# Output-layer weight factors kept whole in DRAM and split on arrival, with later and more buffers for the activated values

## The chip, the cores and the metric

The kernel runs on one core of a Trainium2 chip. The metric is the time of one execution on the device, in microseconds (us), of that core. Before the change three runs took 1200.15, 1204.12 and 1204.95 us; the median is 1204.12 us.

## The reference, cut to what matters

A retention layer (attention with a decay per head) is followed by two feed-forward layers. All inputs are float32.

```python
for t in range(S):                       # B, H, S, D = 4, 8, 768, 64
    state = gamma * state + k[:, :, t] (outer) v[:, :, t]
    y[:, :, t] = scale * q[:, :, t] @ state
x = y reordered to (3072, 512)
h = x @ w_in;  x = maximum(0.01 * h, h) @ w_out          # 512 -> 2048 -> 512
h = x @ w2_in; out = (h * sigmoid(1.702 * h)) @ w2_out   # 512 -> 2048 -> 512
```

## The kernel before, in words

The program is unrolled. It has five stages: the retention layer, then for each of the two feed-forward layers (`lay` 0 and 1) `first` (`x @ w_in` and the activation) and `second` (`g @ w_out`).

Every matrix product is done by Winograd's scheme, with seven products of quarter matrices in place of eight. A quarter product is made of float32 numbers held as two parts, `hi` (rounded to the format `F32R`) and `lo` (the rest), so each takes three matmuls: hi by lo, hi by hi, lo by hi. The weights' seven combinations are called factors here. An SBUF tile `w` holds the factors of one `q` (one eighth of the hidden width) as `[P, 2, 2, 7, P]`: two halves, then hi and lo, then the seven factors of 128 x 128.

**Preparing weights.** `Prep` turns one half of a raw weight tile into seven factors, in steps that `later` runs a given number of ticks after the start: `load` (two DMAs on SP's queue), `words` (two operations of ACT, L122 and L123), `bits` (three of DVE, L127 to L131), `sums` (five of POOL, L136 and L141), `high_part` (ACT's cast to hi, L150), `low_part` (DVE's subtraction, L153) and `store` (L158 and L159, two DMAs of 448 KB to the DRAM tensor `wd`). With a `dest` the parts go straight to a `w` tile and nothing is stored. In `first`, `FAST` sets the ticks of the steps and `line` says which preparations are to come and how many ticks apart (`JIT`, `STORED`). In layer 0 that is 8 of the layer's own input weights 4.25 ticks apart, then the 16 of `w_out` and 8 of the second layer's `w2_in`, all 5.4 apart. In layer 1 it is 8 at 4.25 and the 16 of `w2_out` at 7.5.

**`first`.** The tokens are cut into four blocks of 768, and each into two halves of `T1` = 384 columns. For each block and each `q`, seven products of six matmuls (L410, 128 x 384) are made; after each comes one `tick`. An iteration `n` is one pair (block, q), and two of its seven products belong to the previous `n`. ACT copies and activates (L473; L416 in layer 0, the sigmoid L419 in layer 1), DVE adds banks (L437, L479) and in layer 1 multiplies by the sigmoid (L420). The activated values go into a tile `g` of the pool `g_p` (five buffers) and from there to the DRAM tensor `gd` by a DMA of 192 KB on ACT's queue (L434). In the last block, after the product that is the last to use the input weights of a `q`, `after(q)` takes the `w` tile over for the output weights of that `q` and loads them from `wd` (L692, 1792 KB on SP's queue). Three iterations before the end `prepared` opens the first buffers of `second` and loads eight tiles of `gd` (L536, SP's queue).

**`second`.** Three blocks of 1024 tokens, for each seven products over all eight `q`, 48 matmuls of 128 x 512 (L601). ACT casts each loaded tile to hi (L545) and DVE subtracts for lo (L550) and forms the blocks' sums (L576). The first product (tag `d`) goes through all eight `w` tiles, six matmuls each. Tiles of `gd` are loaded up to 13 items ahead, on SP's queue.

Order and waits: each engine and each DMA queue runs its instructions in the order in which the program issues them. A buffer is reused when the last reader of its former tile is done, for a `g` tile when its store has landed.

```python
            t = g_p.tile([P, T1], F32, tag="g", name="g")          # hidden(), before
    JIT, STORED = 4.25, (5.4, 7.5)
    FAST = (6, 7, 8, 12, 13, 15)
```

Of the kernel before, what the change touches and what calls it, by code (L numbers as in the profile page):

```python
# [9 lines left out]
F32 = mybir.dt.float32  # L10
# [44 lines left out]
class Later:  # L55


    def __init__(self):
        self.now = 0
        self.due = {}  # L60

    def at(self, ticks, step):
        self.due.setdefault(self.now + ticks, []).append(step)

    def tick(self):
        for step in self.due.pop(self.now, []):
            step()
        self.now += 1

    def drain(self):  # L70
        while self.due:
            self.tick()


@with_exitstack
def retention_two_ffn(ctx: ExitStack, tc: tile.TileContext, qkv, consts, small, w1i, w1o, w2i, w2o, scratch, out):
# [4 lines left out]

    wd = {(kind, lay): dram.tile([P, n, 2, 2, 7, P], F32, name=f"wd{kind}{lay}")
          for kind, lay, n in (("o", 0, NQ), ("i", 1, NQ // 2), ("o", 1, NQ))}
    gd = [dram.tile([KF, P, NT], F32, name=f"gd{lay}") for lay in range(2)]
# [6 lines left out]

    later = Later()

    class Prep:
# [288 lines left out]
    def first(lay, wt, blocks, g_p, prep, line, after, prepared):  # L385
# [3 lines left out]
        with ExitStack() as c:  # L389
# [23 lines left out]

            def act(src, dst):
                if lay == 0:
                    nc.scalar.activation(out=dst, in_=src, func=AF.Lrelu)  # L416
                else:
                    s = u_p.tile([P, T1], F32, tag="sg", name="sg", bufs=3)
                    nc.scalar.activation(out=s, in_=src, func=AF.Sigmoid, scale=1.702)  # L419
                    later.at(1, lambda: nc.vector.tensor_tensor(out=dst, in0=src, in1=s, op=ALU.mult))  # L420

            def hidden(n, r, f, src):

                blk, q = pairs[n]
                t = g_p.tile([P, T1], F32, tag="g", name="g")
                ticks = 0 if lay == 0 else 3
                if callable(src):
                    src(t)
                    later.at(1, lambda: act(t, t))
                    ticks += 1  # L430
                else:
                    act(src, t)
                cols = slice((2 * blk + r) * T1, (2 * blk + r + 1) * T1)
                later.at(ticks, lambda: nc.scalar.dma_start(out=gd[lay][f * NQ + q][:, cols], in_=t))  # L434

# [5 lines left out]
            for n in range(len(pairs) + 1):  # L441
# [57 lines left out]
                if now:  # L499
                    product(cur["a"], n, 2, False)  # L500
                    hidden(n, 0, 0, cur["a"])
                    form(2)
                    tick(free)
                    product(cur["b"], n, 7, False)
                    hidden(n, 1, 1, lambda t: add(t, cur["b"], cur["p"]))
                    form(7)
                    tick(free)
# [176 lines left out]

    def loader(kind, lay, n):

        tiles = []

        def after(q):
            t = w_tile(q)  # L690
            if q < n:
                nc.sync.dma_start(out=t.bitcast(F32), in_=wd[kind, lay][:, q])  # L692
            tiles.append(t)

        return tiles, after

    JIT, STORED = 4.25, (5.4, 7.5)

    line = ([(p, w1[p.q], JIT) for p, _ in line] + [(p, None, STORED[0]) for p in preps("o", 0)]
            + [(p, None, STORED[0]) for p in preps("i", 1)[:NQ]])  # L700
# [11 lines left out]

    tiles, after = loader("o", 0, NQ)
    first(0, w1, blocks, g_p, prep_p, line, after, lambda: prepared(0))
    right.close()
    tiles1, after = loader("i", 1, NQ // 2)
    right = ExitStack()
# [10 lines left out]
    g_p = right.enter_context(tc.tile_pool(name="g", bufs=5, side="right", reuse_waits="tile"))  # L728
    F_BUFS = 2
    ctx_p = ExitStack()  # L730
# [4 lines left out]
    for _ in range(3):  # L735
        later.tick()
    line = [(p, tiles1[p.q], JIT) for p in preps("i", 1)[NQ:]] + [(p, None, STORED[1]) for p in preps("o", 1)]
    tiles, after = loader("o", 1, NQ)
    first(1, tiles1, blocks, g_p, prep_p, line, after, lambda: prepared(1))
# [68 lines left out]
```

## Time and profile before

| | us |
|---|---|
| median of three runs | 1204.12 |
| the profiled execution | 1204.84 |
| its span (first to last instruction) | 1203.1 |
| TensorE (PE) busy | 1083.9 (90%) |
| VectorE (DVE) busy | 859.9 (71%) |
| ScalarE (ACT) busy | 579.5 (48%) |
| GpSimd (POOL) busy | 350.5 (29%) |
| granted TensorE clock, mean | 0.96 of full |
| moved by DMA | 263.09 MB, mean 219 GB/s |

`first` of layer 0 runs from about 119 to 399 us of the span, `second` of layer 0 to about 653, `first` of layer 1 from about 655 to 953, and `second` of layer 1 to about 1196. Busy shares are averages over these stages. A busy PE is not a PE at its full pace: matmuls are pipelined, and a matmul that is modelled to last longer counts as busy too. So a stage is best judged by its count of matmuls against the time that so many take in an undisturbed stretch.

### The profile page before, as it was taken

Reading aid. Unit: us, or ns where it says so; the run is one execution under the profiler, and the core shown is the slowest. Engines: PE = TensorE matmul, PEld = TensorE weight load, DVE = VectorE, ACT = ScalarE, POOL = GpSimd, SP = SyncE. Lnnn points to the kernel's source line nnn. Section 1 sums busy time; section 2 is a strip of 40 time slices with the busy share of each in tenths; the row PEclk is TensorE's granted clock in tenths of the full one; section 3 lists DMA queues with packets and bytes.
Section 4 is the critical chain, followed back from the end, with each engine's and each line's share of the span. In section 5 each row is a group of like instructions: output and inputs, shape, how many; then the busy total and the mean of one; then the engine's idle time right before and its main releaser. Section 6 shows DMA issues by size and latency. Waiting matters only on the chain. (4 is left out here: it accounts for less than half of the span.)

```text
span 1203.1 us, 17472 instructions
## 1 busy us (share of the span) xinstructions
PE 1083.9 (90%) x6081; PEld 964.0 (80%) x6082; DVE 859.9 (71%) x1290; ACT 579.5 (48%) x967; POOL 350.5 (29%) x386
## 2 busy tenths in 40 slices
PE   8877989889889699999997787989989799999997
PEld 6766978879789577887885787989989688888886
DVE  5898577586763278687785599888884388687684
ACT  1333556666653244544543464565552255545543
POOL 2566475575742000000002275363540000000000
PEclk9988999999999889999999799999999899999999
DMA  8985757979889942625246653878779953624422
GB/s 312 335 310 193 243 166 233 332 252 342 306 275 370 362 162 89 227 70 179 102 140 245 210 184 131 302 241 273 255 255 349 328 171 99 214 71 137 143 71 70
DMA packets 136185, 263.09 MB, mean 219 GB/s; under 512 B 12064, under 2 KB 88352, under 8 KB 130848
## 3 DMA queue, kind: packets, MB, share of 16 engines
q1 hardware_dynamic: 99232, 211.62, 51.2%
q10 hardware_dynamic: 36864, 50.35, 11.6%
q8 instruction: 48, 0.79, 0.3%
q14 instruction: 41, 0.34, 0.1%
HBM read 157.59 MB, written 104.33 MB: 218 GB/s over the span
## 5 line engine op out<-in xcount | busy, mean ns | idle before, releaser
L545 ACT CAST op<-g 128x512 fp32r<-128x512 f32 x336 | 201.9, 622 | 189.4 <-PE f L601 50.4
L410 PE MATMUL b<-xf,w 128*128 128x384 f32 x1152 | 239.3, 353 | 54.2 <-DVE c L437 25.9
L550 DVE TENSOR_TENSOR op<-g,op 128x512 fp32r<-128x512 f32 x336 | 224.0, 689 | 61.3 <-ACT op L545 59.0
L410 PEld LDWEIGHTS b<-xf,w 128*128 128x128 f32 x1152 | 210.6, 195 | 67.6 <-DVE c L437 33.4
L410 PE MATMUL a<-xf,w 128*128 128x384 f32 x768 | 166.0, 352 | 14.8 <-DVE xf L224 10.5
L136 POOL TENSOR_TENSOR f<-f,rnd 128x512 int32<-128x512 int32 x64 | 93.0, 1453 | 241.4 <-DVE f L131 80.0
L410 PEld LDWEIGHTS a<-xf,w 128*128 128x128 f32 x768 | 144.1, 197 | 18.3 <-DVE xf L224 11.4
L576 DVE TENSOR_TENSOR g<-g 128x512 f32<-128x512 f32 x192 | 146.0, 760 | 17.3 <-DMA g<-gd 17.3
L141 POOL TENSOR_TENSOR f<-f 128x128 f32<-128x128 f32 x256 | 150.9, 610 | 10.0
L632 POOL TENSOR_TENSOR u<-u 128x1024 f32<-128x1024 f32 x6 | 16.0, 2671 | 467.3 <-DVE u L632 392.5
L601 PE MATMUL d<-op,w 128*128 128x512 f32 x576 | 140.1, 402 | 12.7 <-DVE op L550 11.6
L410 PE MATMUL c<-xf,w 128*128 128x384 f32 x768 | 150.1, 344 | 0.7 <-DVE xf L224 0.7
L601 PEld LDWEIGHTS d<-op,w 128*128 128x128 f32 x576 | 111.2, 194 | 38.6 <-DVE op L550 14.0
L601 PE MATMUL e<-op,w 128*128 128x512 f32 x576 | 136.3, 393 | 5.6 <-DVE op L550 5.6
L410 PEld LDWEIGHTS c<-xf,w 128*128 128x128 f32 x768 | 139.4, 192 | 2.1 <-DVE xf L224 2.1
L601 PE MATMUL f<-op,w 128*128 128x512 f32 x576 | 132.5, 389 | 0.0
L601 PEld LDWEIGHTS e<-op,w 128*128 128x128 f32 x576 | 108.2, 189 | 29.7 <-DVE op L550 7.3
L601 PEld LDWEIGHTS f<-op,w 128*128 128x128 f32 x576 | 108.1, 188 | 22.5
L153 DVE TENSOR_TENSOR f<-f,hi 128x896 fp32r<-128x896 f32 x40 | 53.8, 1345 | 29.2 <-ACT hi L150 29.0
L437 DVE TENSOR_TENSOR g<-b,p 128x384 f32<-128x384 f32 x64 | 35.3, 552 | 52.9 <-DMA gd<-g 29.0
L601 PE MATMUL h<-op,w 128*128 128x512 f32 x288 | 67.0, 390 | 0.0
L601 PEld LDWEIGHTS h<-op,w 128*128 128x128 f32 x288 | 53.8, 188 | 11.0
(72 smaller groups left out, 1177.1 us busy)
## 6 DMA issues: line engine op xcount, KB each, us to landing
gd<-g ACTq DMA_DIRECT2D x256, 192.0 KB, 3.9
g<-gd SPq DMA_DIRECT2D x192, 256.0 KB, 4.4
w<-wdo SPq DMA_DIRECT2D x16, 1792.0 KB, 9.5
in<-qkv SPq DMA_DIRECT2D x21, 1024.0 KB, 6.5
wdo<-hi SPq DMA_DIRECT2D x32, 448.0 KB, 3.3
wdo<-f SPq DMA_DIRECT2D x32, 448.0 KB, 3.3
xr<-xd SPq DMA_DIRECT2D x7, 1536.0 KB, 8.4
raw<-w1i SPq DMA_DIRECT2D x32, 256.0 KB, 5.7
```

The lines of the kernel that those rows point to most:

```text
L136: nc.gpsimd.tensor_tensor(out=self.f.bitcast(I32), in0=self.f.bitcast(I32), in1=r, op=ALU.add)
L141: nc.gpsimd.tensor_tensor(out=f[:, o], in0=f[:, a], in1=f[:, b], op=ALU.subtract)
L153: nc.vector.tensor_tensor(out=self.lo, in0=self.t.bitcast(F32)[:, 1:], in1=self.hi.bitcast(F32), op=ALU.subtract)
L410: nc.tensor.matmul(out=t, lhsT=w[:, k, a], rhs=x[:, b, k], start=(start and m == 0), stop=(m == 5), skip_group_check=True)
L437: nc.vector.tensor_tensor(out=o, in0=x, in1=y, op=ALU.add)
L545: nc.scalar.copy(out=t[:, 0], in_=block_of(raw, *item))
L550: nc.vector.tensor_tensor(out=t[:, 1], in0=block_of(raw, *item), in1=t[:, 0].bitcast(F32), op=ALU.subtract)
L576: nc.vector.tensor_tensor(out=a(*s[0]), in0=a(*s[1]), in1=a(*s[2]), op=s[3])
L601: nc.tensor.matmul(out=t[:, j], lhsT=w[:, j, a], rhs=x[:, b], start=(new and q == 0 and m == 0), stop=(q == NQ - 1 and m == 2), skip_group ...
L632: put = lambda o, x, y, op=ALU.add, e=nc.vector: e.tensor_tensor(out=o, in0=x, in1=y, op=op)
```

## The change

1. The factors of the two output weights (`kind` "o") lie in DRAM as whole float32: `wd["o", lay]` is `[P, NQ, 2, 7, P]`, half as large. Their preparation ends with `sums`; `store_whole` writes one 448 KB tile, and neither `high_part` nor `low_part` is run.
2. `load_second` loads those 896 KB into the `lo` half of the `w` tile, and `split` makes hi by a cast on ACT (L729) and lo by a subtraction on DVE (L730), in place. The casts are due 5 and 6 ticks after the load, each subtraction one tick after its cast. A second `Later`, `loads`, counts those ticks along with `later` and is not drained at the end of `first`, so that the last splits run in the first steps of `second`.
3. In layer 0 `g_p` has seven buffers in place of five. In layer 1 it stays at five, but the tile is taken when DVE's product is issued, one tick after the sigmoid.
4. The `hi` tile of stored input factors comes from the ring of `f` tiles, which has 4 buffers in place of 3 (layer 0) and 3 in place of 2 (layer 1).
5. The pace: `JIT` 4 in place of 4.25; `STORED` 4.6 for `w_out`, 6.5 for `w2_in` and 7.5 for `w2_out`, in place of 5.4, 5.4 and 7.5. In `FAST` `low_part` is due at 14 in place of 13, a store at 16 in place of 15 (a whole store at 14).

```diff
     def tick(self):
 ...
         self.now += 1
+        for other in self.along:
+            other.tick()
 
     def drain(self):
+        along, self.along = self.along, ()
         while self.due:
             self.tick()
+        self.along = along
...
-    wd = {(kind, lay): dram.tile([P, n, 2, 2, 7, P], F32, name=f"wd{kind}{lay}")
-          for kind, lay, n in (("o", 0, NQ), ("i", 1, NQ // 2), ("o", 1, NQ))}
+    wd = {("i", 1): dram.tile([P, NQ // 2, 2, 2, 7, P], F32, name="wdi1")}
+    for lay in range(2):
+        wd["o", lay] = dram.tile([P, NQ, 2, 7, P], F32, name=f"wdo{lay}")
...
-    later = Later()
+    loads = Later()
+    later = Later((loads,))
...
-                self.hi = self.pool.tile([P, 7, P], F32R, tag="hi", name="hi", bufs=2)
+                self.hi = self.pool.tile([P, 8, P], U32, tag="f", name="hi", bufs=F_BUFS).bitcast(F32R)[:, 1:]
...
+        def store_whole(self):
+            nc.sync.dma_start(out=wd["o", self.lay][:, self.q, self.hh], in_=self.t.bitcast(F32)[:, 1:])
...
             later.at(at[2], self.sums)
+            if self.kind == "o":
+                later.at(at[4], self.store_whole)
+                return
...
-    FAST = (6, 7, 8, 12, 13, 15)
+    FAST = (6, 7, 8, 12, 14, 16)
...
+                def gate(src, t):
                     s = u_p.tile([P, T1], F32, tag="sg", name="sg", bufs=3)
                     nc.scalar.activation(out=s, in_=src, func=AF.Sigmoid, scale=1.702)
...
+                    def product():
+                        dst = tile() if t is None else t
+                        nc.vector.tensor_tensor(out=dst, in0=src, in1=s, op=ALU.mult)
+                        later.at(2, lambda: store(dst))
+
+                    later.at(1, product)
...
+    def load_second(lay):
+        tiles = []
+
+        def after(q):
+            t = w_tile(q)
+            nc.sync.dma_start(out=t[:, :, 1].bitcast(F32), in_=wd["o", lay][:, q])
+            tiles.append(t)
+
+            def split(h):
+                hi, lo = t[:, h, 0], t[:, h, 1]
+                nc.scalar.copy(out=hi, in_=lo.bitcast(F32))
+                loads.at(1, lambda: nc.vector.tensor_tensor(out=lo, in0=lo.bitcast(F32), in1=hi.bitcast(F32),
+                                                            op=ALU.subtract))
+
+            for h in range(2):
+                loads.at(5 + h, lambda h=h: split(h))
+
+        return tiles, after
...
-    JIT, STORED = 4.25, (5.4, 7.5)
+    JIT, STORED = 4, (4.6, 6.5, 7.5)
...
-    F_BUFS = 3
-    g_p = right.enter_context(tc.tile_pool(name="g", bufs=5, side="right", reuse_waits="tile"))
+    F_BUFS = 4
+    g_p = right.enter_context(tc.tile_pool(name="g", bufs=7, side="right", reuse_waits="tile"))
```

How the instructions move, at three places. Line numbers differ between the two programs: L437, L479, L420, L550 and L576 of before are L459, L501, L444, L572 and L598 now; L127, L129 and L131 are L134, L136 and L138.

The first place is DVE in layer 0's `first`, while the output weights are prepared (`f` is a preparation's working tile, `hi` its upper part; `b`, `c` are PSUM banks, `p` a copy). Before:

```order
L479 COPY p<-c 128x384
L127 TENSOR_SCALAR f<-f 128x512
L129 TENSOR_SCALAR f<-f 128x512
L131 SCALAR_TENSOR_TENSOR f<-raw,f 128x512
L437 TENSOR_TENSOR c<-b,p 128x384
L437 TENSOR_TENSOR g<-b,p 128x384
L153 TENSOR_TENSOR f<-f,hi 128x896
```

Now:

```order
L501 COPY p<-c 128x384
L459 TENSOR_TENSOR c<-b,p 128x384
L134 TENSOR_SCALAR f<-f 128x512
L136 TENSOR_SCALAR f<-f 128x512
L138 SCALAR_TENSOR_TENSOR f<-raw,f 128x512
L459 TENSOR_TENSOR g<-b,p 128x384
```

The long subtraction over 896 columns has left this place; the rest is the same.

The second place is DVE in the last block of layer 1's `first`, one iteration near its end (`sg` is the sigmoid, `op` an operand of `second`). Before:

```order
L479 COPY p<-c 128x384
L420 TENSOR_TENSOR g<-g,sg 128x384
L437 TENSOR_TENSOR c<-b,p 128x384
L420 TENSOR_TENSOR g<-c,sg 128x384
L420 TENSOR_TENSOR g<-b,sg 128x384
L437 TENSOR_TENSOR g<-b,p 128x384
L420 TENSOR_TENSOR g<-a,sg 128x384
```

Now:

```order
L501 COPY p<-c 128x384
L444 TENSOR_TENSOR g<-g,sg 128x384
L459 TENSOR_TENSOR c<-b,p 128x384
L444 TENSOR_TENSOR g<-c,sg 128x384
L730 TENSOR_TENSOR w<-w 128x896 x2
L444 TENSOR_TENSOR g<-b,sg 128x384
L459 TENSOR_TENSOR g<-b,p 128x384
L444 TENSOR_TENSOR g<-a,sg 128x384
```

Two subtractions of a split stand in each such iteration, ahead of the products for banks `b` and `a`.

The third place is DVE at the start of layer 1's `second`. Before:

```order
L550 TENSOR_TENSOR op<-g,op 128x512 x4
L576 TENSOR_TENSOR g<-g 128x512
L550 TENSOR_TENSOR op<-g,op 128x512
L576 TENSOR_TENSOR g<-g 128x512
L550 TENSOR_TENSOR op<-g,op 128x512
```

Now:

```order
L572 TENSOR_TENSOR op<-g,op 128x512 x3
L730 TENSOR_TENSOR w<-w 128x896
L572 TENSOR_TENSOR op<-g,op 128x512
L598 TENSOR_TENSOR g<-g 128x512
L730 TENSOR_TENSOR w<-w 128x896
L572 TENSOR_TENSOR op<-g,op 128x512
```

These are the splits of the seventh `w` tile; the two of the eighth follow a few rows further on, so four subtractions stand among the first operations of `second`.

## Rows read from the trace of the kernel before

**Rows 1.** Page, 40 equal slices: tenths of granted clock and DMA's busy share.

```profile
PEclk9988999999999889999999799999999899999999
DMA  8985757979889942625246653878779953624422
```

**Rows 2.** Stretches of the span: us; busy us (instructions) of PE, PEld, DVE, ACT, POOL; clock; DMA.

```profile
190.00:355.00 165.00, 148.06 (x799) 142.87 (x798) 115.15 (x157) 99.08 (x173) 99.96 (x114) 0.98 0.85 294
355.00:399.40 44.40, 39.37 (x211) 38.41 (x210) 16.17 (x27) 18.46 (x36) 6.81 (x10) 0.96 1.01 370
399.40:427.00 27.60, 17.33 (x49) 12.73 (x49) 8.16 (x14) 6.25 (x12) 0.00 (x0) 0.72 0.88 347
...
735.00:890.00 155.00, 142.15 (x772) 137.83 (x771) 133.93 (x210) 89.08 (x157) 75.67 (x85) 0.98 0.72 247
890.00:953.40 63.40, 55.04 (x279) 53.27 (x277) 27.43 (x54) 19.36 (x39) 3.75 (x7) 0.89 0.95 342
953.40:980.00 26.60, 25.27 (x109) 20.28 (x110) 19.20 (x32) 13.65 (x23) 0.00 (x0) 1.00 0.75 258
```

**Rows 3.** The chain that ended last, in order of time: start us, us, what.

```profile
886.03 2.12 PE c L410 x12
...
891.50 8.50 DMA gd<-g
...
930.53 14.02 DMA gd<-g
...
966.48 10.88 PE e L601 x48
```

**Rows 4.** What PE waited for, 355 to 427 us: total us, times, longest.

```profile
PE d L601 <- DVE op L550: 10.3, 3, 6.6
PE b L410 <- ACT b L473: 5.0, 3, 3.9
```

**Rows 5.** Timeline of SP's queue, 365 to 425 us: start us, us, issues.

```profile
383.68 8.79 SPq L536 DMA_DIRECT2D g<-gd  x8
393.32 10.17 SPq L692 DMA_DIRECT2D w<-wdo  x4
407.74 17.28 SPq L536 DMA_DIRECT2D g<-gd  x12
```

**Rows 6.** DMA issues, 355 to 427 us: count, KB each, median us to landing.

```profile
DMA packets 8969, 26.01 MB, mean 361 GB/s; under 512 B 941, under 2 KB 5162, under 8 KB 8069
...
w<-wdo SPq DMA_DIRECT2D x7, 1792.0 KB, 9.7
...
wdi<-f SPq DMA_DIRECT2D x3, 448.0 KB, 8.4
```

**Rows 7.** DMA issues, 890 to 965 us, the same columns.

```profile
w<-wdo SPq DMA_DIRECT2D x8, 1792.0 KB, 9.5
gd<-g ACTq DMA_DIRECT2D x31, 192.0 KB, 8.3
```

**Rows 8.** Groups of DVE and ACT, 190 to 355 us: busy us, mean ns, idle before.

```profile
L153 DVE TENSOR_TENSOR f<-f,hi 128x896 fp32r<-128x896 f32 x21 | 29.1, 1387 | 19.9 <-ACT hi L150 19.8
...
L150 ACT CAST hi<-f 128x896 fp32r<-128x896 f32 x21 | 19.8, 944 | 25.3 <-POOL f L141 23.4 <-issue 1.0 <-ACT g L416 0.5
```

**Rows 9.** What PE waited for, 190 to 355 us.

```profile
PE b L410 <- DVE xf L224: 7.7, 3, 3.3
PE b L410 <- DVE c L437: 5.4, 5, 1.4
PE b L410 <- ACT b L473: 3.7, 4, 2.1
```

**Rows 10.** What PE waited for, 735 to 890 us.

```profile
PE b L410 <- DVE c L437: 6.4, 5, 2.4
```

**Rows 11.** Groups of DVE and ACT, 890 to 953.4 us, POOL nearly idle.

```profile
L153 DVE TENSOR_TENSOR f<-f,hi 128x896 fp32r<-128x896 f32 x1 | 1.1, 1082 | 0.0
...
L150 ACT CAST hi<-f 128x896 fp32r<-128x896 f32 x1 | 0.9, 942 | 1.0 <-POOL f L141 1.0
```

More of the change, by code (lines that the diff above doesn't have):

```diff
@@ L55, with __init__ @@
 class Later:
-    def __init__(self):
+    def __init__(self, along=()):
         self.now = 0
         self.due = {}
+        self.along = along
     def at(self, ticks, step):
@@ L68, in tick @@
         self.now += 1
+        for other in self.along:
+            other.tick()
     def drain(self):
+        along, self.along = self.along, ()
         while self.due:
             self.tick()
+        self.along = along
 @with_exitstack
@@ L412, in product, with hidden, relu @@
                         m += 1
-            def act(src, dst):
-                if lay == 0:
+            def hidden(n, r, f, src=None, made=None):
+                blk, q = pairs[n]
+                cols = slice((2 * blk + r) * T1, (2 * blk + r + 1) * T1)
+                tile = lambda: g_p.tile([P, T1], F32, tag="g", name="g")
+                store = lambda t: nc.scalar.dma_start(out=gd[lay][f * NQ + q][:, cols], in_=t)
+                def relu(src, dst):
                     nc.scalar.activation(out=dst, in_=src, func=AF.Lrelu)
-                else:
+                    store(dst)
+                def gate(src, t):
                     s = u_p.tile([P, T1], F32, tag="sg", name="sg", bufs=3)
                     nc.scalar.activation(out=s, in_=src, func=AF.Sigmoid, scale=1.702)
[L420 to L430, printed above, removed]
-                else:
-                    act(src, t)
-                cols = slice((2 * blk + r) * T1, (2 * blk + r + 1) * T1)
-                later.at(ticks, lambda: nc.scalar.dma_start(out=gd[lay][f * NQ + q][:, cols], in_=t))
+                    def product():
[3 more added lines that the diff above has]
+                    later.at(1, product)
+                if made is not None:
+                    t = tile()
+                    made(t)
+                    later.at(1, lambda: relu(t, t) if lay == 0 else gate(t, t))
+                elif lay == 0:
+                    relu(src, tile())
+                else:
+                    gate(src, None)
             def add(o, x, y):
@@ L504, in first @@
                     product(cur["b"], n, 7, False)
-                    hidden(n, 1, 1, lambda t: add(t, cur["b"], cur["p"]))
+                    hidden(n, 1, 1, made=lambda t: add(t, cur["b"], cur["p"]))
                     form(7)
@@ L683, in second, with load_first @@
             later.drain()
-    def loader(kind, lay, n):
+    def load_first(n):
         tiles = []
@@ L691, in after @@
             if q < n:
-                nc.sync.dma_start(out=t.bitcast(F32), in_=wd[kind, lay][:, q])
+                nc.sync.dma_start(out=t.bitcast(F32), in_=wd["i", 1][:, q])
             tiles.append(t)
         return tiles, after
-    JIT, STORED = 4.25, (5.4, 7.5)
+    def load_second(lay):
[13 more added lines that the diff above has]
+    JIT, STORED = 4, (4.6, 6.5, 7.5)
     line = ([(p, w1[p.q], JIT) for p, _ in line] + [(p, None, STORED[0]) for p in preps("o", 0)]
-            + [(p, None, STORED[0]) for p in preps("i", 1)[:NQ]])
+            + [(p, None, STORED[1]) for p in preps("i", 1)[:NQ]])
     left = ExitStack()
     early = []
-    F_BUFS = 3
-    g_p = right.enter_context(tc.tile_pool(name="g", bufs=5, side="right", reuse_waits="tile"))
+    F_BUFS = 4
+    g_p = right.enter_context(tc.tile_pool(name="g", bufs=7, side="right", reuse_waits="tile"))
     ctx_p = ExitStack()
@@ L711, in prepared @@
         early.append(Early(left, lay))
-    tiles, after = loader("o", 0, NQ)
+    tiles, after = load_second(0)
     first(0, w1, blocks, g_p, prep_p, line, after, lambda: prepared(0))
     right.close()
-    tiles1, after = loader("i", 1, NQ // 2)
+    tiles1, after = load_first(NQ // 2)
     right = ExitStack()
@@ L728, in retention_two_ffn @@
     g_p = right.enter_context(tc.tile_pool(name="g", bufs=5, side="right", reuse_waits="tile"))
-    F_BUFS = 2
+    F_BUFS = 3
     ctx_p = ExitStack()
@@ L736, in retention_two_ffn @@
         later.tick()
-    line = [(p, tiles1[p.q], JIT) for p in preps("i", 1)[NQ:]] + [(p, None, STORED[1]) for p in preps("o", 1)]
-    tiles, after = loader("o", 1, NQ)
+    line = [(p, tiles1[p.q], JIT) for p in preps("i", 1)[NQ:]] + [(p, None, STORED[2]) for p in preps("o", 1)]
+    tiles, after = load_second(1)
     first(1, tiles1, blocks, g_p, prep_p, line, after, lambda: prepared(1))
```

## Prediction

> **What bounds the kernel now.** I first looked at the slices of the page: the clock is at its full level except for dips, and DMA is busiest just where the dips at 390 to 430 and at 930 us are [rows 1]. So the next view was the busy time by stretch [rows 2], against the time that the same matmuls take undisturbed. The chain gives that pace: 12 matmuls of `first` in 2.12 us, so 0.1767 us each, and 48 of `second` in 10.88 us, so 0.2267 us [rows 3]. Count times pace, taken from the length of the stretch, is what it loses, lost clock included [rows 2]:
>
> - 190 to 355 us (layer 0, weights prepared): 165.0 - 799 x 0.1767 = 23.8 us
> - 355 to 399.4 (end of its `first`): 44.4 - 211 x 0.1767 = 7.1
> - 399.4 to 427 (the first product of its `second`): 27.6 - 49 x 0.2267 = 16.5
> - 735 to 890 (layer 1, weights prepared): 155.0 - 772 x 0.1767 = 18.6
> - 890 to 953.4 (end of its `first`): 63.4 - 279 x 0.1767 = 14.1
> - 953.4 to 980 (start of its `second`): 26.6 - 109 x 0.2267 = 1.9
>
> That is 82 us. In the four stretches at the ends of `first` (39.6 us) the cause is transfers. From 891 to 953 us the chain consists mostly of stores of `g`: six waits, of which the first and the longest are shown, 8.50 and 14.02 us [rows 3]. A store of 192 KB took 8.3 us there, beside weight loads of 1792 KB at 9.5 us [rows 7]. DVE cannot write the next `g` until a store has landed. In layer 0 DMA is full (share 1.01 and 0.88) [rows 2] and moves 26.0 MB from 355 to 427 us [rows 6]. PE waits 10.3 us for operands of `second` and 5.0 us for ACT's copy [rows 4]. SP's queue shows why: the eight tile loads begin at 383.7 us, four weight loads stand behind them until 403.5, and the next twelve tile loads come only from 407.7 on [rows 5].
>
> In the two stretches with preparations DVE and ACT hold PE up, each for a different thing [rows 9, 10]. ACT spent 23.4 us of idle time waiting for POOL before its 21 casts to hi, and DVE then 19.8 us waiting for those casts [rows 8]. Each runs in order, so copies and sums that PE wants stand behind them.
>
> **The change part by part.** *Bytes at the end of `first`.* Each output weight load falls from 1.835 to 0.918 MB: seven in 355 to 427 us, so 26.0 - 6.4 = 19.6 MB there. At the measured 361 GB/s that takes 54 us [rows 6], while PE's own work in the two stretches is 37.3 + 11.1 = 48.4 us, and more of `second` can run in the time won. So layer 0 goes from overfull to nearly full. The last preparation also starts earlier: 8 x 4 + 16 x 4.6 + 8 x 6.5 = 157.6 ticks in place of 8 x 4.25 + 24 x 5.4 = 163.6, six ticks of six matmuls (1.06 us), 6.4 us. Its stores then leave SP's queue before the tile loads of 383.7 us. Seven buffers in place of five let a store in layer 0 take 7/5 as long before it holds ACT. In layer 1 the tile is held one tick less.
>
> Of layer 0's 23.6 us I leave 7: 2.5 for the splits (below) and 4.5 because the last preparations still overlap with the first loads. That is -16.6 us (bounds -6, if only the stores' waits of 7.1 us go, and -20). Of layer 1's 16.0 I leave 4, since there the preparations add less: -12 (bounds -4 and -14).
>
> Against this stands the size of the transfer. In these rows time to landing hardly goes with size: 9.5 us for 1792 KB, 8.4 for 448 KB, 8.3 for 192 KB [rows 6, 7]. They all stand in one crowd, so fewer bytes shorten every wait, and that is what I take. The Trainium skill (DMA: Bandwidth & Descriptors, Rules for kernel authors) asks for at least 1 MiB in one DMA, and the new load falls below that. Its section on the anatomy of one DMA has a fit (2.0 us and the bytes at 436 GB/s, made on another queue kind): an estimate by it is 6.2 us before and 4.1 after, so 2.1 us back for each load where halving at the measured pace gives 2.5, some 7 us less over 16 loads and a sum of 1175.
>
> *The split.* Nothing is added in total: 32 casts (0.94 us) and 32 subtractions are no longer made in the preparation and are made on arrival. While POOL works a subtraction takes 1.39 us [rows 8], while it rests 1.08 [rows 11]. What hides them: in the last block of layer 1 DVE is busy 27.4 and ACT 19.4 of 63.4 us [rows 2]; six tiles add 12 x 1.08 = 13.0 and 12 x 0.94 = 11.3 us, and neither comes near the undisturbed 49.3 us. Two tiles fall into the start of `second`: four subtractions, 4.3 us. DVE is idle there for 26.6 - 19.2 = 7.4 us, about half of it in the first product, so PE waits between 0.6 and 4.3 us. I take 2.5 in each layer, counted above. The cast adds a wait: it is due five products after the load's issue, 5.3 us, and ACT's copies for PE stand behind it. Half of 9.5 us is 4.75, inside that; 8.4 us, as the 448 KB stores took, would not be.
>
> *The preparation.* Of the 21 casts in 190 to 355 us all but some five were for output weights. With them goes ACT's wait for POOL and DVE's for ACT; now only SP's store waits for POOL. What is late next is `words`, which overwrites the buffer that POOL's first operation still reads, and at 4.6 ticks (4.9 us) it comes sooner than at 5.4. PE's waits for `xf` (7.7 us) belong to a change of block and stay. Those for sums and copies are 5.4 + 3.7 [rows 9], and 6.4 in layer 1 [rows 10]; I take half: -4.5 and -3.2. The bounds are far apart: the whole 42.4 us less the 7.7 of `xf` on one side, and on the other +5 for the denser pace.
>
> *The first eight preparations* keep all their operations and stand 4 ticks apart in place of 4.25. The same work a little earlier: 0 (±4). The third and fourth `f` buffers only remove waits.
>
> **Sum.** 1204.84 - 16.6 - 12 - 4.5 - 3.2 = 1168.5 us on the profiled execution. That is 0.7 above the median of the three runs, so 1168. A difference of 0.5% (6 us) is about what a measurement of this kernel can tell from none.
>
> **The rivals.** *Only the stores' waits go.* The first product of `second` stays late, since the tile loads still stand behind four weight loads on SP's queue [rows 5], and four subtractions are new in front of it. Then layer 0 gives 7.1, layer 1 10, less 5 for the splits, and the preparation 7.7: 1185 us. Against it: those four loads halve. 20%.
>
> *The preparation was the larger part.* If ACT's and DVE's waits [rows 8] were behind all that those stretches lose but the waits for `xf`, 42.4 less 7.7 for each layer, 27 us go in place of 7.7: 1149 us. For it: PE's waits listed make up only 16.8 of the 23.8 us lost, the rest follows them. 13%.
>
> *Slower: the cast waits for its weights.* If a load still lands after 9.5 us [rows 7], each of 16 loads holds ACT 4.2 us, 67 us in place of the 39.6 lost there now; with the preparation's 7.7 back that is 1225 us. It decides from 16 x (landing - 5.3) = 39.6 + 7.7, a landing of 8.3 us. Against it: a quarter of the bytes of that stretch are gone. 5%.
>
> *Nothing is won.* If the waits follow the number of transfers in flight and not their bytes, the ends stay and the splits take 5 of the preparation's 7.7 us: 1202 us. For it: times hardly depend on size [rows 6, 7]. 5%.
>
> **How the numbers follow.** The forecast (1155 to 1180 by its own bounds) has 57%. The range 1145 to 1190 takes in the forecast and most of the first two rivals. Faster by over 0.5%: 57 + 20 + 13 = 90%; within it 5%; slower 5%.
>
> **What would show it.** Right: DMA's share below 0.9 in the last blocks, weight loads landing in under 5.3 us, no chain of `g` stores, and the first product of layer 0's `second` in under 16 us in place of 27.6; DVE with 16 long subtractions fewer per preparing stretch and no waits of ACT for POOL outside input weights. Wrong: ACT's split cast waiting for the weight load with PE behind it, or stretches with preparations that lose as much as before.

## The result, and the profile after

The changed kernel takes 1185.72 us (median of four runs, 1182.95 to 1186.46). The kernel before took 1203.93 in the runs beside it. The ratio is 0.985, with a 95% interval of 0.9823 to 0.9877: 18 us, or 1.5%, faster. The forecast was 1168 us.

First the slices, the answer to [rows 1]:

```profile
PEclk9888998999999989999999799999999999999999
DMA  8886565978769632723434573866659823524322
```

Of the clock's dips at the ends of `first` (slices 14, 15 and 32 before) one slice is left, the 15th. DMA's digit there fell from 9 to 6 in slice 14 and from 9 to 8 in slice 32; the slices just ahead of them, 13 and 31, still read 9. Next the stretches of the program as in [rows 2], with the same columns. The ends of the stages fall on the same matmul as before, give or take one; the other bounds lie up to 26 matmuls apart, so of each stretch its own count is read:

```profile
192.50:357.50 165.00, 148.93 (x792) 144.89 (x791) 100.33 (x147) 91.62 (x163) 92.08 (x115) 0.96 0.76 254
357.50:401.60 44.10, 40.32 (x217) 39.43 (x216) 23.75 (x33) 24.18 (x42) 3.04 (x5) 0.96 0.86 296
401.60:421.30 19.70, 13.24 (x50) 9.17 (x49) 12.92 (x19) 9.98 (x16) 0.00 (x0) 0.93 0.78 252
724.20:881.00 156.80, 146.24 (x801) 143.34 (x800) 120.98 (x202) 78.36 (x147) 74.89 (x86) 0.98 0.65 211
881.00:928.50 47.50, 44.99 (x254) 44.34 (x253) 35.28 (x58) 25.33 (x45) 4.47 (x7) 1.00 0.82 275
928.50:957.00 28.50, 23.63 (x96) 18.45 (x95) 21.35 (x32) 15.98 (x25) 0.00 (x0) 0.94 0.65 217
```

DVE has lost 14.8 us of work in the stretch with layer 0's preparations (100.33 in place of 115.15), yet its 165 us hold no more matmuls than before (792 in place of 799). Layer 1's end has full clock (1.00 in place of 0.89). The last row, the start of layer 1's `second`, is worse than before: clock 0.94 in place of 1.00.

For a finer comparison I cut `first` by iterations, 42 matmuls each (the first has 30, and the last 12 are counted to the end), and took from each stretch its count of matmuls times the undisturbed pace, as the prediction does. The table gives the loss in us, one profile each; e1, e2, e4, e12 and e13 are experiments below, in a word each.

| stretch | before | after | e1 old format | e2 old pace | e4 spread | e12 twice | e13 u first |
|---|---|---|---|---|---|---|---|
| layer 0, iterations 0 to 7 | 11.2 | 11.3 | 11.6 | 12.2 | 11.6 | 11.5 | 11.4 |
| 8 to 23 | 18.9 | 20.1 | 35.1 | 14.0 | 19.5 | 21.9 | 21.7 |
| 24 to the end | 12.5 | 11.3 | 8.9 | 17.3 | 8.4 | 21.9 | 7.4 |
| first product of `second` | 16.6 | 8.8 | 12.4 | 9.5 | 7.8 | 8.5 | 6.4 |
| layer 1, 0 to 2 | 13.6 | 14.1 | 13.6 | 13.2 | 14.3 | 13.4 | 7.3 |
| 3 to 7 | 14.7 | 8.0 | 8.5 | 14.8 | 8.2 | 9.0 | 8.0 |
| 8 to 23 | 13.7 | 11.6 | 17.6 | 5.5 | 10.6 | 11.4 | 10.9 |
| 24 to the end | 18.4 | 6.0 | 20.1 | 8.3 | 5.7 | 17.0 | 4.5 |
| first product of `second` | 2.1 | 6.0 | 3.5 | 5.7 | 6.4 | 9.0 | 6.0 |

From before to after these nine stretches lose 24.5 us less. The retention stage ahead, whose code is the same, took 119.0 us in the one profile and 121.5 in the other, and the rests of the two `second` 1.2 and 1.1 us more: the span is 19.9 us shorter. Differences of 1 to 2 us in one cell are therefore not read.

The gains lie at the ends, as forecast: 9.0 us in layer 0 (the first product of `second` 7.8 of it) and 12.4 in layer 1, of which its first product gives 3.9 back. The rest is 6.7 us in iterations 3 to 7 of layer 1. Iterations 8 to 23 of layer 0 gain nothing.

What landed when, 355 to 430 us and then 865 to 950 us, the answers to [rows 6] and [rows 7]. Ahead of them stands the row of layer 0's stores before, from the view of [rows 6]:

```profile
gd<-g ACTq DMA_DIRECT2D x24, 192.0 KB, 7.5
```

```profile
DMA packets 9578, 19.58 MB, mean 261 GB/s; under 512 B 967, under 2 KB 4196, under 8 KB 9572
...
w<-wdo SPq DMA_DIRECT2D x6, 896.0 KB, 6.4
gd<-g ACTq DMA_DIRECT2D x25, 192.0 KB, 4.9
```

```profile
w<-wdo SPq DMA_DIRECT2D x8, 896.0 KB, 5.4
gd<-g ACTq DMA_DIRECT2D x35, 192.0 KB, 4.1
```

The bytes come to the 19.6 MB forecast, though this window is 3 us longer than that of before and holds six weight loads in place of seven. The loads land after 6.4 and 5.4 us in place of 9.7 and 9.5, the stores after 4.9 and 4.1 in place of 7.5 and 8.3 (medians). But 5.4 and 6.4 are more than the 5.3 us after which the split's cast is due. What PE waits for at layer 0's end, the answer to [rows 4], from 357.5 to 428 us, and then at layer 1's, from 881 to 957 us:

```profile
PE b L423 <- ACT b L495: 3.7, 1, 3.7
PE d L623 <- DVE op L572: 2.9, 2, 2.6
PE d L623 <- DVE w L730: 2.8, 2, 2.2
```

```profile
PE d L623 <- DVE w L730: 3.4, 2, 2.2
PE b L423 <- ACT b L495: 1.6, 1, 1.6
```

`L730` is the split's subtraction. The wait for ACT's copy comes from the split's cast, which stood ahead of it in ACT's queue and waited for its weights (the group of that line, 357.5 to 428 us):

```profile
L729 ACT CAST w<-w 128x896 fp32r<-128x896 f32 x14 | 12.8, 940 | 7.2 <-DMA w<-wdo 5.6 <-ACT g L435 1.6
```

Why that load was late, SP's queue shows (340 to 425 us, the answer to [rows 5]):

```profile
369.81 0.37 SPq L724 DMA_DIRECT2D w<-wdo  x1
370.23 10.06 SPq L558 DMA_DIRECT2D g<-gd  x8
380.65 21.53 SPq L724 DMA_DIRECT2D w<-wdo  x4
402.22 17.57 SPq L558 DMA_DIRECT2D g<-gd  x16
```

The eight tile loads of `prepared` still go out in one piece ahead of the fifth weight load; that load was issued at 380.65, some 3.4 us after its turn (one comes every iteration, 42 matmuls or 7.4 us, and the fourth went out at 369.81), and landed 7.9 us later, in the crowd of the eight.

### The profile page after: what moved, and what is told of

It is laid out like the page before. It is cut to its first block, busy times and chain, and to the rows that moved or that the text cites. A ratio compares the mean times of both kernels' runs of the same rounds, so it can differ in the third digit from the quotient of the medians.

```text
span 1183.2 us, 17426 instructions
## 1 busy us (share of the span) xinstructions
PE 1082.1 (91%) x6082; PEld 965.8 (82%) x6082; DVE 851.5 (72%) x1290; ACT 578.6 (49%) x967; POOL 342.6 (29%) x386
## 4 chain that ended last, share of the span: by engine, by line
PE 53%; DVE 7%; DMA 7%; ACT 3%; issue 3%; POOL 2%; ACTq 1%; POOLq 0%; SPq 0%; DVEq 0%
PE f L623 11%; PE d L623 9%; PE e L623 9%; PE b L423 8%; PE h L623 6%; PE a L423 5%; PE c L423 4%; DMA gd<-g 2%; DMA w<-wdo 2%; DMA xd<-u 1%; DVE xf L237 1%; DVE g L598 1%; DMA g<-gd 1%; DMA raw<-w2i 1%; POOL f L148 1%
## 5 line engine op out<-in xcount | busy, mean ns | idle before, releaser
L423 PE MATMUL b<-xf,w 128*128 128x384 f32 x1152 | 238.9, 353 | 40.5 <-DVE xf L237 13.8
L572 DVE TENSOR_TENSOR op<-g,op 128x512 fp32r<-128x512 f32 x336 | 225.2, 691 | 62.2 <-ACT op L567 61.1
L423 PEld LDWEIGHTS b<-xf,w 128*128 128x128 f32 x1152 | 211.7, 196 | 52.4 <-DVE c L459 18.4
L423 PE MATMUL a<-xf,w 128*128 128x384 f32 x768 | 163.3, 349 | 14.3 <-DVE xf L237 10.0
L143 POOL TENSOR_TENSOR f<-f,rnd 128x512 int32<-128x512 int32 x64 | 87.1, 1361 | 232.3 <-DVE f L138 110.2
L598 DVE TENSOR_TENSOR g<-g 128x512 f32<-128x512 f32 x192 | 146.6, 764 | 4.7 <-DMA g<-gd 4.3
L623 PE MATMUL d<-op,w 128*128 128x512 f32 x576 | 136.6, 393 | 11.3 <-DVE w L730 6.2
L623 PE MATMUL e<-op,w 128*128 128x512 f32 x576 | 139.9, 400 | 4.4 <-DVE op L572 4.4
L623 PEld LDWEIGHTS d<-op,w 128*128 128x128 f32 x576 | 108.0, 189 | 36.8 <-DVE w L730 8.2
L623 PEld LDWEIGHTS e<-op,w 128*128 128x128 f32 x576 | 110.9, 194 | 29.4 <-DVE op L572 6.3
L134 DVE TENSOR_SCALAR f<-f 128x512 f32<-128x512 f32 x64 | 36.8, 575 | 48.0 <-ACT f L130 36.7
L129 ACT ACTIVATE rnd<-raw 128x512 int16<-128x512 uint32 x64 | 50.7, 792 | 28.0 <-POOL f L143 10.9
```

The lines of the kernel that those rows point to most:

```text
L129: nc.scalar.activation(out=rnd[:, :, 0], in_=raw[:, :, 0], func=AF.Copy, scale=2.0**-29)
L134: nc.vector.tensor_scalar(out=f.bitcast(F32), in0=f.bitcast(F32), scalar1=HW_MIN, scalar2=HW_MAX, op0=ALU.max, op1=ALU.min)
L143: nc.gpsimd.tensor_tensor(out=self.f.bitcast(I32), in0=self.f.bitcast(I32), in1=r, op=ALU.add)
L423: nc.tensor.matmul(out=t, lhsT=w[:, k, a], rhs=x[:, b, k], start=(start and m == 0), stop=(m == 5), skip_group_check=True)
L572: nc.vector.tensor_tensor(out=t[:, 1], in0=block_of(raw, *item), in1=t[:, 0].bitcast(F32), op=ALU.subtract)
L598: nc.vector.tensor_tensor(out=a(*s[0]), in0=a(*s[1]), in1=a(*s[2]), op=s[3])
```

## The experiments

All are compared with the kernel before, run on the same chip beside them, by ratio with its 95% interval.

**e1, the old format alone.** Factors stored and loaded as two parts, so without the split on arrival; all else as changed.

```diff
-            if self.kind == "o":
-                later.at(at[4], self.store_whole)
-                return
...
-            nc.sync.dma_start(out=t[:, :, 1].bitcast(F32), in_=wd["o", lay][:, q])
+            nc.sync.dma_start(out=t.bitcast(F32), in_=wd["o", lay][:, q])
```

> The output weights' factors are stored and loaded as two parts again (1792 KB a load, no split on arrival); buffers, the gate's late tile and the pace stay as changed. Theory A (the bytes at the ends of `first` were the bound): the weight loads land after 9 us again, the stretches at the ends of `first` lose some 35 us again, and the time is 1198 to 1206 us. Theory B (the buffers and the later tile took the stores' waits away): the ends of `first` keep most of their gain and the time is 1185 to 1193 us.

Measured: 1212.49 us, ratio 1.0065 (1.0043 to 1.0088), slower than before, and beyond what either theory gave. The end of layer 1 loses 20.1 us again and the first product in layer 0 12.4, so the buffers and the pace alone do not keep the gain of layer 1. In layer 0 they nearly do: its end and that product lose 8.9 + 12.4 = 21.3 us, against 29.1 before and 20.1 with the change. Loads and stores land late again with as many loads as in the change (355 to 435 us):

```profile
w<-wdo SPq DMA_DIRECT2D x8, 1792.0 KB, 9.8
gd<-g ACTq DMA_DIRECT2D x31, 192.0 KB, 7.7
```

What neither theory had: iterations 8 to 23 of layer 0 lose 35.1 us in place of 18.9. These 16 us are not the new pace alone. All stored preparations now take their `hi` tile from the ring of `f` tiles too, and ACT waits there for the stores of `hi` to land (188 to 346 us), a wait that the same window of the kernel before has for 0.2 us only:

```profile
ACT hi L156 <- DMA wdo<-hi: 9.6, 6, 3.3
```

How much of the 16 us is pace and how much the ring, no run separates.

**e2, the old pace alone.** `JIT` 4.25, `STORED` 5.4, 5.4, 7.5, and `FAST` of before, in the changed kernel.

```diff
-    FAST = (6, 7, 8, 12, 14, 16)
+    FAST = (6, 7, 8, 12, 13, 15)
...
-    JIT, STORED = 4, (4.6, 6.5, 7.5)
+    JIT, STORED = 4.25, (5.4, 5.4, 7.5)
```

> The changed kernel with the pace of before: 4.25, 5.4, 5.4 and 7.5 ticks and the old ticks of the last steps. Theory C (the denser pace of layer 0 gives back what the shorter preparation frees): layer 0's iterations 8 to 23, which lose 20 us in the changed kernel, lose 12 or less, and the time is 1176 to 1181 us. Theory A alone: the last preparations reach further into the last block, its loads crowd, and the time is 1186 to 1192 us.

Measured: 1185.99 us, 0.9845 (0.9818 to 0.9873): the same as the change. Theory C named a real loss: iterations 8 to 23 lose 14.0 in place of 20.1 us in layer 0 and 5.5 in place of 11.6 in layer 1. But theory A's crowd comes too: 17.3 in place of 11.3 from 24 to the end of layer 0, 8.3 in place of 6.0 in layer 1, and layer 1's iterations 3 to 7 lose 14.8 again. The pace moves losses from one place to the other; on the whole it is not where the 18 us come from. Of the 9.0 us won at layer 0's ends, though, 6.7 are the pace's: with the old one they lose 17.3 + 9.5 = 26.8 us.

**e3, five buffers.** `g_p` with five buffers in layer 0, the gate's tile taken ahead of the sigmoid.

```diff
-    g_p = right.enter_context(tc.tile_pool(name="g", bufs=7, side="right", reuse_waits="tile"))
+    g_p = right.enter_context(tc.tile_pool(name="g", bufs=5, side="right", reuse_waits="tile"))
...
-                        dst = tile() if t is None else t
+                        dst = t
...
-                    gate(src, None)
+                    gate(src, tile())
```

> The changed kernel with five buffers in both layers, the tile taken ahead of the sigmoid as before. Theory B: the waits for stores come back at the ends of both `first` stages, 8 us or more, 1193 us or more. Theory A: stores land in some 4 us once the bytes are halved, five buffers are enough, and the time is 1184 to 1189 us.

Measured: 1182.03 us, 0.9813 (0.9778 to 0.9849); its interval overlaps that of the change. That is below the range of either theory, and theory B falls: with stores that land in some 4 us the buffers are worth nothing that can be measured.

**e12, each weight load made twice.** The bytes of before in the new order of work.

```diff
-            nc.sync.dma_start(out=t[:, :, 1].bitcast(F32), in_=wd["o", lay][:, q])
+            for m in range(2):
+                nc.sync.dma_start(out=t[:, :, m].bitcast(F32), in_=wd["o", lay][:, q])
```

> The changed kernel, with each output weight load made twice: the same 896 KB go to the lo half and to the hi half of the tile (the cast overwrites the latter), so the bytes at the ends of `first` are those of before while the preparation, the split, the buffers and the pace stay as changed. If the halved bytes are what the ends of `first` gain from: the two ends and starts of `second`, which lose 32 us in the changed kernel, lose 45 or more, and the time is 1197 us or more. If the gain is the smaller preparation's: 1186 to 1190 us.

Measured: 1206.16 us, 1.0022 (1.0003 to 1.0041): the whole gain is gone. The four stretches at the ends lose 21.9 + 8.5 + 17.0 + 9.0 = 56.4 us in place of 32.1. Its loads, 355 to 430 us, and what ACT waited for, 357 to 430 us:

```profile
w<-wdo SPq DMA_DIRECT2D x13, 896.0 KB, 8.4
g<-gd SPq DMA_DIRECT2D x24, 256.0 KB, 5.7
gd<-g ACTq DMA_DIRECT2D x25, 192.0 KB, 6.3
```

```profile
ACT w L730 <- DMA w<-wdo: 19.8, 5, 9.6
```

(Line 730 is the cast in this kernel.) With twice the bytes ACT waits 19.8 us for weights, and PE behind it. In e12 the number of loads doubles too, and a cast waits for both of its tile's loads; e1 has the old bytes in the old number of loads and no cast behind them. At layer 1's ends both lose the gain (20.1 + 3.5 = 23.6 us in e1 and 26.0 in e12, in place of 12.0), so there it is the bytes that decide. At layer 0's ends only e12 does (30.4 us in place of 20.1; e1 21.3), so what the bytes cost there, they cost through the cast that waits for them. e12 also shows the wait of the forecast's slower rival, 19.8 us here and 20.7 in layer 1, but it does not confirm that rival's sum. The sum had its break-even at a landing of 8.3 us, and single loads land after 8.4 and 7.5 us here; but a tile is complete only 9.5 and 10.3 us (medians) after its first load is issued, for which the sum gives 16 x 4.6 = 74 us of waits in place of the 40.5 measured. That the time comes out at that of before, as at the break-even, is chance.

**e4, tile loads spread.** The eight loads of `prepared` go out two ticks apart, so that weight loads go between them.

```diff
-            for item in ITEMS[:NQ]:
-                load_block(lay, self.raw, {"x": self.x}, *item)
+            for n, item in enumerate(ITEMS[:NQ]):
+                later.at(2 * n, lambda item=item: load_block(lay, self.raw, {"x": self.x}, *item))
```

> The changed kernel with the eight tile loads for `second` issued two ticks apart in place of all at once ahead of the fifth weight load. If those loads are what makes the fifth weight load land after 7.9 us and holds ACT's cast 5.6 us (layer 0) and 4.4 us (layer 1): the cast's wait falls under 2 us, the last three iterations of layer 0 lose 2 us in place of 5.5, and the time is 1178 to 1183 us. Rival (the loads only move the crowd to the start of `second`): what the last iterations win, the first product of `second` loses, and the time is 1184 to 1188 us.

Measured: 1176.38 us, 0.9762 (0.9737 to 0.9788), 9 us faster than the change (10.6 by the two ratios), more than expected. The last three iterations of layer 0 lose 1.5 us in place of 5.5 and those of layer 1 1.7 in place of 3.0. The cast's group, in the same part of the program (357 to 428 us), waits 2.4 us for weights in place of 5.6:

```profile
L729 ACT CAST w<-w 128x896 fp32r<-128x896 f32 x14 | 12.8, 940 | 4.0 <-DMA w<-wdo 2.4 <-ACT g L435 1.6
```

The fifth weight load now goes out 7.4 us after the fourth (369.28 and 376.70) and lands after 5.3 us. So the order on SP's queue was the cause of what the end of layer 0 still lost; layer 1's 1.3 us are within what is not read. The stretches of the table explain 5 of the 9 us; the rest is not placed.

**e6, the last splits on POOL.** On top of e4, the four subtractions of the last two weight tiles.

```diff
-                loads.at(1, lambda: nc.vector.tensor_tensor(out=lo, in0=lo.bitcast(F32), in1=hi.bitcast(F32),
-                                                            op=ALU.subtract))
+                e = nc.gpsimd if q >= 6 else nc.vector
+                loads.at(1, lambda: e.tensor_tensor(out=lo, in0=lo.bitcast(F32), in1=hi.bitcast(F32),
+                                                    op=ALU.subtract))
```

> The kernel with spread tile loads (1176.4 us), and the four subtractions of the last two weight tiles of each layer made by POOL, which rests there. If DVE's order is what holds the first product of `second` (PE waits 3.0 and 1.2 us for a split's subtraction, and 2.7 us in each layer for an operand behind it): that product loses 4 us and 3 us in place of 7.8 and 6.4, and the time is 1168 to 1172 us. Rival (the weights or the tiles of `gd` land too late, whoever subtracts): POOL's slower subtraction comes on top, and the time is 1176 to 1180 us.

Measured: 1180.24 us, 0.9817 (0.9794 to 0.9839), as the rival had it: the first products lose 8.3 and 8.4 us in place of 7.8 and 6.4. POOL takes twice as long (385 to 430 us):

```profile
L731 POOL TENSOR_TENSOR w<-w 128x896 fp32r<-128x896 f32 x4 | 8.8, 2221 | 43.0 <-ACT w L729 43.0
```

That is 2.22 us in place of DVE's 1.09. And DVE's own operations of 128 x 512 that begin while POOL subtracts take 2.0 to 2.6 us in place of 0.69. The timelines of POOL and DVE (399 to 414 us) show it twice:

```profile
406.88 2.09 POOL L731 TENSOR_TENSOR w<-w 128x896 fp32r<-128x896 f32 x1 [3.06 <-ACT w L729]
411.16 2.10 POOL L731 TENSOR_TENSOR w<-w 128x896 fp32r<-128x896 f32 x1 [2.20 <-ACT w L729]
```

```profile
407.51 2.00 DVE L598 TENSOR_TENSOR g<-g 128x512 f32<-128x512 f32 x1 [1.68 <-DMA g<-gd]
411.24 2.57 DVE L598 TENSOR_TENSOR g<-g 128x512 f32<-128x512 f32 x1
```

So the work did not leave DVE's path, and PE's waits moved instead of going: 2.7 us for ACT's casts, 2.5 for DVE's operands and 1.4 for POOL, after 3.0 for the subtraction and 2.7 for operands in e4. Whether DVE's order binds that product this run can't tell.

**e7, the old ticks of the last steps.** `FAST` of before, with the new pace.

```diff
-    FAST = (6, 7, 8, 12, 14, 16)
+    FAST = (6, 7, 8, 12, 13, 15)
```

> The changed kernel with `low_part` at tick 13 and a store at 15 as before, and the new pace kept. Layer 1's iterations 3 to 7 lose 8.0 us in the changed kernel and 14.8 with both old ticks and old pace. If one tick more between the cast and the subtraction is what DVE gains from: they lose 13 to 15 us again and the time is 1190 to 1194 us. If it is the earlier start of the first eight preparations (4 ticks): they keep 8 to 9 us and the time is 1184 to 1187 us.

Measured: 1185.26 us, 0.9858 (0.9835 to 0.9881). Iterations 3 to 7 of layer 1 lose 10.1 us, against 8.0 with the change and 14.8 with old pace and old ticks. The time follows the second theory; the 10.1 us lie between the two. Of those 6.8 us 4.7 come from starting the first eight preparations 4 ticks apart; the 2.1 left for the tick are hardly more than what is not read. The same start costs as much further on: in layer 1 it is all that differs in pace between e7 and e2, and its iterations 8 to 23 lose 11.4 us in e7 and 5.5 in e2.

**e8, e10, e11, e9: the pace of layer 0, once the loads are spread.** e8 is e4 with `STORED` 5.4 and 5.4, e10 the same with `FAST` of before, e11 has 5.0 and 6.5, e9 is e8 with e6's POOL.

```diff
-    JIT, STORED = 4, (4.6, 6.5, 7.5)
+    JIT, STORED = 4, (5.4, 5.4, 7.5)
```

> The kernel with spread tile loads (1176.4 us), and layer 0's stored preparations 5.4 ticks apart as before, the first eight 4 apart. If the denser pace costs what the two old-pace runs show: iterations 16 to 23 of layer 0 lose 4 to 5 us in place of 9.0; if the last preparations, now 4 ticks later, do not crowd the last block once the tile loads are spread, the rest stays and the time is 1170 to 1173 us. Rival: iterations 24 to the end lose 5 us more, as with the old pace, and the time is 1175 to 1179 us.

> Spread tile loads, stored preparations 5.4 ticks apart, first eight 4 apart, `low_part` at 13 and stores at 15. With stores at 16 iterations 16 to 23 of layer 0 lost 14.9 us at this pace, with stores at 15 and the first eight 4.25 apart 4.5. If the tick of the last steps decides: they lose 4 to 6 us and the time is 1168 to 1174 us. If the phase against the change of block decides (first eight 4 in place of 4.25 apart): 10 us or more and 1178 to 1186 us.

> Spread tile loads and `w_out`'s preparations 5.0 ticks apart in place of 4.6, all else as in the kernel with spread tile loads (1176.4 us). If a denser pace costs by its density: iterations 8 to 23 of layer 0 lose 16 to 18 us in place of 19.5 and the time is 1173 to 1176 us. If single collisions of a preparation's steps with a change of block decide: a step to either side, 1172 to 1186 us, and the loss moves between iterations instead of shrinking in all.

> All three together: spread tile loads, the last splits' subtractions on POOL, stored preparations 5.4 ticks apart. If their effects add: 1162 to 1168 us. If the start of `second` is bound by landings and the last block by the late preparations: 1175 us or more.

| run | us | ratio (95%) | layer 0, iterations 8 to 15 | 16 to 23 |
|---|---|---|---|---|
| e4 (4.6, 6.5) | 1176.38 | 0.9762 (0.9737 to 0.9788) | 10.5 | 9.0 |
| e8 (5.4, 5.4) | 1185.95 | 0.9871 (0.9847 to 0.9895) | 7.3 | 14.9 |
| e10 (5.4, 5.4, old ticks) | 1184.57 | 0.9845 (0.982 to 0.987) | 6.9 | 15.9 |
| e11 (5.0, 6.5) | 1181.01 | 0.9809 (0.9785 to 0.9832) | 7.4 | 12.3 |
| e9 (5.4, 5.4, POOL) | 1185.91 | 0.9862 (0.982 to 0.9904) | 7.1 | 16.8 |

All my hopes for a slacker pace were wrong, and e8 is slower than either of its theories had it. The slacker pace does take 3 us from iterations 8 to 15, but 16 to 23 lose 3 to 8 us more. In e2, with 5.4 and 5.4 too but the first eight 4.25 apart, those same iterations lost 4.5. In this stretch e10 differs from e2 in that start alone, and loses 15.9. So density is not the measure there; which step of a preparation meets the change of block is. The groups of e8 from 262 to 345 us show the meeting point, and below them stands the same group and window of e2:

```profile
L157 ACT CAST hi<-f 128x896 fp32r<-128x896 f32 x5 | 4.7, 942 | 3.3 <-POOL f L148 2.9 <-ACT g L435 0.4
...
L236 ACT CAST xf<-xt 128x768 fp32r<-128x768 f32 x4 | 3.3, 834 | 11.3 <-POOL xt L235 10.9 <-ACT g L435 0.4
```

```profile
L236 ACT CAST xf<-xt 128x768 fp32r<-128x768 f32 x4 | 3.3, 835 | 1.2 <-ACT g L435 1.2
```

ACT waits 10.9 us before four casts of the new block's operands, for POOL, which is busy with a preparation's sums; in e2 the same four casts do not wait for POOL at all.

**e13, the pool of results first.** SP's waits in e4, 390 to 430 us, named one more cause:

```profile
SPq L558 <- DMA gd<-g: 6.9, 1, 6.9
```

The second tile load of `second` waited 6.9 us for the landing of the last store of `g`: its buffer lies where `g`'s buffers were. So the pool of result tiles, needed only after eight steps, is opened first and gets that place.

```diff
-            y_p, o_p, u_p = pool("y2", NQ), pool("op2", HIGH), pool("u2", 4)
+            u_p, y_p, o_p = pool("u2", 4), pool("y2", NQ), pool("op2", HIGH)
```

> The kernel with spread tile loads (1176.4 us), and the pool of result tiles of `second` opened ahead of the pools of tiles and operands, so that it is the result tiles, needed last, that lie where the buffers of `g` were. In the run with spread loads SP's second tile load for `second` of layer 0 waited 6.9 us for the landing of the last store of `g`. If that wait is what the first product of `second` loses: SP's wait goes, the product loses 4 us and 4 us in place of 7.8 and 6.4, and the time is 1168 to 1173 us. Rival (the landing of the last weight tile and the splits behind it hold that product anyway): it loses 7 and 6 us again and the time is 1174 to 1179 us.

Measured: 1169.23 us, 0.9733 (0.9715 to 0.9751), the fastest of all. The time is as expected, the reason only in part. SP's wait for the store is gone (390 to 430 us, all rows):

```profile
SPq L724 <- PE b L423: 8.8, 2, 4.5
SPq L558 <- DMA w<-wdo: 2.6, 1, 2.6
SPq L558 <- DMA g<-gd: 1.5, 4, 0.6
```

Yet the first products still lose 6.4 and 6.0 us, as the rival said: PE now waits 3.1 us for the last splits and 2.1 for operands (395 to 420 us):

```profile
PE d L623 <- DVE w L730: 3.1, 2, 1.9
PE d L623 <- DVE op L572: 2.1, 2, 1.2
```

The larger part, 7.0 us, is in layer 1's iterations 0 to 2. There, in the changed kernel, a cast of an `xf` operand waited for the store of a result tile (636 to 675 us, first the change, then e13):

```profile
ACT xf L236 <- DMA xd<-u: 8.0, 1, 8.0
```

```profile
ACT L440 <- DMA xd<-u: 4.5, 1, 4.5
```

What PE waited for in the same window, again first the change, then e13:

```profile
PE a L423 <- DVE xf L237: 10.0, 2, 7.1
```

```profile
PE a L423 <- issue: 2.9, 1, 2.9
PE b L423 <- ACT b L495: 1.0, 1, 1.0
PE a L423 <- DVE xf L237: 0.4, 1, 0.4
```

With the result tiles elsewhere, the wait falls on the line of a later sigmoid (L440), 4.5 us, and of it 1.0 us reaches PE, through ACT's copy behind it.

## Why the prediction was right and where it was not

The time lies in the range and the sign was forecast with 90%; the size was twice what came: 36.3 us of gain forecast, 18 measured, and 1186 us is above the forecast's own bounds (1155 to 1180). Part of this is luck. The terms that the sum was made of brought 9.0 + 8.5 + 0.9 = 18.4 us in the profiles, 6.7 came from a term put at 0, and some 5 went in stages with the same code. Without the 6.7 the time would be some 1192 us, outside the range. By its steps:

- **What bounds the ends of `first`: right in layer 1, in part in layer 0.** In layer 1 it is bytes, as e1 and e12 show by giving them back, and not buffers (e3). In layer 0 the old bytes alone cost little (e1), and 6.7 of the 9.0 us won are the pace's (e2). The forecast had a part of this in the last preparation, which ends earlier; that this is how the pace works there is argued, not shown. Loads and stores both landed in about half to two thirds of their times with half the weight bytes.
- **The size against the number of transfers.** A weight load came back by 3.3 to 4.1 us (9.7 to 6.4, 9.5 to 5.4), more than the 2.5 of the measured pace. An estimate by the fit in the Trainium skill (DMA: Bandwidth & Descriptors, the anatomy of one DMA) is 4.1 us for the new load and 2.1 back; no load here landed in so little at the median, which I put down to the crowd it stands in. That the new load falls below the 1 MiB which the Trainium skill asks for (the same page, Rules for kernel authors) has a cost that no run here shows by itself: e12 moves the old bytes in 896 KB loads and takes the time of before, but its casts wait for them as well.
- **Layer 0's ends: -16.6 forecast, -9.0 measured.** The bounds held (-6 to -20). The step that failed is "Its stores then leave SP's queue before the tile loads", taken to be enough: the preparation's stores were out of the way, but the eight tile loads themselves stood before the fifth weight load, which went out late, landed after 7.9 us and held ACT (e4 takes 4.0 us off the last three iterations). The condition of the slower rival, a landing above 5.3 us, was met by single loads.
- **Layer 1's ends: -12 forecast, -8.5 measured** (12.4 less 3.9 in the first product). The split's cost was 2.5 us by my sum; PE's waits for the subtractions are 2.8 and 3.4 us. Right in kind, and a little small.
- **The preparation: -7.7 forecast, -0.9 measured** (+1.2 in layer 0, -2.1 in layer 1). This is the step that failed most. I took half of PE's waits for sums and copies and set the denser pace beside it as a bound of +5. The runs show both, and larger: at the old pace (e2) the smaller preparation is worth 18.9 - 14.0 = 4.9 us in layer 0 and 13.7 - 5.5 = 8.2 in layer 1, and the new pace takes 20.1 - 14.0 = 6.1 and 11.6 - 5.5 = 6.1 back. At the new pace the part removed, with its use of the `f` ring, was worth 35.1 - 20.1 = 15 us in layer 0; that the new `f` buffers "only remove waits" did not hold in e1. "What is late next is `words`" is in part borne out: DVE waits longer for it (192.5 to 357.5 us; 8.1 us for the same line in the kernel before), but the waits for `hi` ahead of it are mostly gone, and no row shows PE held by `words`. What else grew is ACT's wait for POOL's `xt` at the changes of block (1.1 us before):

```profile
L134 DVE TENSOR_SCALAR f<-f 128x512 f32<-128x512 f32 x20 | 10.8, 542 | 27.1 <-ACT f L130 18.9 <-POOL f L148 8.0
...
L236 ACT CAST xf<-xt 128x768 fp32r<-128x768 f32 x8 | 6.7, 832 | 8.0 <-POOL xt L235 7.2 <-ACT g L435 0.8
```

- **The first eight preparations: 0 (±4) forecast.** In layer 0 nothing; in layer 1 6.7 us of gain, of which e7 puts 4.7 on the pace. That is outside the bound, on the good side; the loss that the same start brings further on (e7) stands under the preparation.
- **The rivals.** "Only the stores' waits go" had 1185 us, the number that came, with the first product of `second` still late and for the reason it named (loads behind loads on SP's queue, splits in front), though that product did shorten by 7.8 us. It had the number by other terms: 12.1 us from the ends with the splits taken off and 7.7 from the preparation, where 17.5 and 0.9 were measured. "The preparation was the larger part" fell: 0.9 us went there, and 13.1 at the old pace. The slower rival's wait is seen in e12, its break-even not.
- **What would show it.** DMA's share fell below 0.9 (0.86 and 0.82), as said. The chain of stores is gone from layer 1; in layer 0 the chain that ended last still passes through two landings of `g` stores, of 6.5 and 7.9 us (from 374.0 and 403.1 us). Weight loads under 5.3 us and a first product under 16 us were not reached (5.4 and 6.4 us; 19.7 us). Both signs of being wrong came: the split's cast waited 5.6 us for a weight load with PE 3.7 us behind it, and layer 0's stretch with preparations lost as much as before (20.1 and 18.9 us).

## What to carry to other kernels

When halved bytes relieve a crowded stretch, read next the order in which the queue issues what is left: here eight loads that nobody needed yet stood before one that held an engine, and spreading them gave half as much again as the change. Work taken out of an in-order stage is worth what the pace leaves of it; change the pace in a run of its own, and the buffers too (e1 mixes them). And where one pool's buffers lie over another's, the new pool's first use waits for the old one's last store: give that place to what is needed last.

## What was not expected of the hardware

Time to landing had hardly gone with size in the kernel before (8.3 to 9.5 us for 192 to 1792 KB), but it went with the bytes of the whole crowd: stores whose size did not change landed in 4.1 in place of 8.3 us, and in 8.1 again in e1 (899 to 977 us), with as many loads and the old bytes. A subtraction of 128 x 896 takes POOL 2.22 us, twice DVE's 1.09, and DVE's operations of 128 x 512 that began while it ran took 2.0 to 2.6 us in place of 0.69 (e6).
